# Sliding-window attention and a gated layer on one core: k's transposing DMA directly behind q's, and v spread earlier on GpSimd

## The chip, the cores and the metric

The kernel runs on one core of a Trainium2 chip. The metric is the device time of one execution in microseconds, the median of several runs. TensorE is written PE in the profile, VectorE DVE, ScalarE ACT, GpSimd POOL, and the queue from which SyncE issues DMAs SPq.

## The reference, cut to what matters

```python
# q, k, v: (8, 8, 576, 64) float32;  w_in: (512, 2048);  w_out: (2048, 512)
scores = q @ k.transpose(0, 1, 3, 2) / sqrt(64)
scores = where(0 <= row - column < 64, scores, -1e9)   # a causal window of 64
attn = exp(scores - max); attn = attn / (sum(attn) + 1e-9)
x = (attn @ v).transpose(0, 2, 1, 3).reshape(4608, 512)
h = x @ w_in
out = (h * cos(h)) @ w_out
```

There are eight batches of eight heads. Each row of 576 sees only itself and the 63 rows ahead of it, so attention is done in blocks of 64 rows (nine to a batch, numbered j = 0 to 8), each against 128 columns.

## The kernel before, in words

The second part, the layer, sets the shape. The 4608 rows of x are cut into nine row tiles of 512, numbered `mt`; each is one stage of the program. A stage has two halves. In the first, 16 column blocks `ff` of h are made by 64 matmuls (L359); ScalarE takes the sine of each (`sin`, L504) and VectorE multiplies it with h (`gT`, L507). In the second, 64 matmuls with w_out (L519) make the output (`out_ps`), which VectorE and ScalarE copy and SyncE stores.

Attention is threaded through these stages, one batch ahead. A planner holds a list of steps with due times: `at(time, function, ...)` enters one, and `pump(time)` emits all steps that are due, in order of time. A stage is T = 32 units of that time: the first 16 are one for each `ff`, the other 16 one for each four matmuls of the output. The due times decide only the order in which instructions stand in each engine's queue; on the chip every engine takes its queue in order, and semaphores hold an instruction until what it reads is there.

For batches b = 2 to 7 (t0 = 32(b - 1) is the start of the stage in which batch b's scores are made), the steps that matter here are these:

- `load_chunk` (L146): GpSimd issues the loads of q and of k, five chunks each, one stage ahead.
- `turn` (L213): SyncE issues a transposing DMA which turns the loaded rows of q or k (two of them: chunks 0 to 3, and chunk 4) into `qX` and `kX`, with the head dimension on the partitions.
- `spread_q` (L221): VectorE copies `qX` in four pieces into `qB`, a block layout with zeros between the two heads of a pair.
- `load_v` (L152): GpSimd issues five loads of v at the head of the stage.
- `spread_v` (L112, tile `v`): GpSimd makes, in two copies, the tiles of v that begin at odd multiples of 64.
- the scores of a group of 3 or 4 blocks (L263, tile `s_ps`) on TensorE, from about 14.6 units into the stage; then maximum on VectorE (L286), exponential on ScalarE (L297), reciprocal `rden` on VectorE (L304), the normalised weights `w` on GpSimd (L311), and a transposing DMA `wT` on SyncE (L323). There are 10 groups in a stage, 12 in the first.
- `values` (L338, tile `o_ps`) and `put_x` (tile `xT`) at the end of the stage: they use the weights of the blocks that belong to the next row tile, and the next stage's h matmuls wait for `xT`. One of the four `xT` copies is ScalarE's.
- `clear` (L367): in the stage of batch 2 alone, GpSimd sets `qB`'s second buffer to zero in four pieces.

In this kernel the turn of q for b > 2 stands at t0 - 5.8, near the end of the stage ahead; that of k stands at t0 + 0.2. For b = 2 they stand at 18.6 and 32.2. `spread_q` begins at t0 + 4.2 and `spread_v` at t0 + 24.2, among the `w` products.

Of the kernel before, what the change touches and what calls it, by code (L numbers as in the profile page):

```python
# [58 lines left out]
def kernel(  # L59
# [326 lines left out]
    def at(time, fn, *args):  # L386
        plan.append((time, len(plan), fn, args))
# [25 lines left out]
    for b in range(1, B):  # L413
        t0 = T * (b - 1)
        if b == 1:
            for p in range(PAIRS):
                for lag, fn in ((0, tr_q), (0.01, tr_k), (0.02, put_q), (0.03, put_k)):
                    at(7 + 1.8 * p + lag, fn, b, p)
        else:
            for i, name in enumerate(("q", "k")):  # L420
                for c in range(NC):
                    at(4 + 0.5 * (c + NC * i) if b == 2 else t0 - T + 4.9 + 0.9 * (c + NC * i), load_chunk, name, b, c)
                for c, (lo, hi) in enumerate(((0, 4), (4, 5))):
                    at((t0 + 0.2 if i else 18.6 if b == 2 else t0 - 5.8) + 0.1 * c, turn, name, b, lo, hi)
            for c, (lo, hi) in enumerate(((0, 4), (4, 5))):
                for h in range(2):
                    at(t0 + 4.2 + h + 2 * c, spread_q, b, h, lo, hi)
            for c in range(5):
                at(t0 + 0.4 + 0.9 * c, load_v, b, c)
            for half in range(2):  # L430
                at(t0 + 24.2 + 0.1 * half, spread_v, b, half)
    for half in range(2):
        at(17.5, spread_v, 1, half, "dma")
    for p in range(PAIRS):
# [32 lines left out]
    turn, turn_h = iter(range(100)), iter(range(100))  # L467
# [17 lines left out]
    for mt in range(n_mt):  # L485
# [23 lines left out]
        half = n_ff // 2 if mt == 0 else n_ff  # L509
# [49 lines left out]
```

## Time and profile before

| what | value |
|---|---|
| median of 3 runs | 349.0 us (347.15 to 350.04) |
| the profiled execution | 350.49 us, its span 348.7 us |
| mean granted TensorE clock | 0.961 of full speed |
| PE busy | 306.8 us, 88% of the span |
| ACT busy | 238.0 us, 68% |
| DVE busy | 225.2 us, 65% |
| POOL busy | 194.1 us, 56% |
| HBM read and written | 36.70 MB and 9.44 MB |

The span runs from the first to the last instruction of the profiled execution; 1.8 us of its time lie outside it. Busy time on an engine does not say that the engine is what everything waits for: the four engines are interlocked, and the stages have different limits. In rows of a timeline the bracket at the end gives the time for which the engine sat idle ahead of that row and what released it; "x4" says that several like instructions are merged in one row.

### The profile page before, as it was taken

To read this page: it belongs to the slowest core of one execution; us is meant where nothing else is said; L and a number is where in the kernel's file an instruction comes from. 1 tells how busy PE (TensorE), PEld (TensorE's weight loads), DVE (VectorE), ACT (ScalarE), POOL (GpSimd) and SP (SyncE) were. 2 spreads that over 40 slices of the span, in tenths; PEclk is the share of its full clock that TensorE was granted. 3 is DMA by queue.
4 is the path that set the end of the run, shared out by engine and by line. 5 is a ranking of instruction groups with operands and counts; after the bars stand their busy time and mean duration, and the time that the engine had idled before them with its cause. 6 is when DMAs were issued, how large, how long until landed. Compare 5 with 4: busy or idle time off the path is not lost.

```text
span 348.7 us, 7499 instructions
## 1 busy us (share of the span) xinstructions
PE 306.8 (88%) x2452; PEld 153.7 (44%) x2452; DVE 225.2 (65%) x850; ACT 238.0 (68%) x785; POOL 194.1 (56%) x215
## 2 busy tenths in 40 slices
PE   3989999899988599928998299956999999999996
PEld 2644554435543255404553155423554545454443
DVE  5876897698669275935769166772759867723821
ACT  4897799569967498735977279763987998513610
POOL 9993176896898079922898049950791292000000
PEclk9989999999999899987999799996999999999999
DMA  7999999999399945999399992999369535111002
GB/s 95 179 210 207 187 163 126 104 200 170 61 133 158 223 58 104 117 154 184 65 118 144 163 133 58 148 157 207 65 57 198 157 60 137 50 62 61 0 33 89
DMA packets 165960, 43.56 MB, mean 125 GB/s; under 512 B 155104, under 2 KB 161440, under 8 KB 165920
## 3 DMA queue, kind: packets, MB, share of 16 engines
q0 software_dynamic: 99632, 18.36, 70.6%
q1 hardware_dynamic: 66144, 24.52, 36.8%
q8 instruction: 19, 0.31, 0.4%
q14 instruction: 21, 0.17, 0.2%
q10 hardware_dynamic: 144, 0.20, 0.2%
HBM read 36.70 MB, written 9.44 MB: 132 GB/s over the span
## 4 chain that ended last, share of the span: by engine, by line
PE 46%; DMA 18%; POOL 15%; DVE 9%; issue 8%; ACT 3%; POOLq 0%; SPq 0%; DVEq 0%
PE out_ps L519 22%; PE h_ps L359 17%; DMA kX<-k 11%; POOL w L311 5%; DMA v<-in_v_dram 4%; POOL v L112 4%; DVE gT L507 2%; PE s_ps L263 2%; ACT e L297 2%; POOL v L152 2%; DVE s L286 1%; DMA k<-in_k_dram 1%; DMA wT<-w 1%; PE o_ps L338 1%; POOL q L146 1%
## 5 line engine op out<-in xcount | busy, mean ns | idle before, releaser
L519 PE MATMUL out_ps<-w_out,gT 128*128 128x512 bf16 x560 | 139.2, 392 | 0.0
L359 PE MATMUL h_ps<-xT,w_in 128*128 128x512 bf16 x576 | 129.2, 382 | 1.5 <-DVE xT L112 0.6
L297 ACT ACTIVATE e<-s,negm 128x128 f32<-128x128 f32 x256 | 98.8, 390 | 30.7 <-DVE negm L286 30.7
L311 POOL TENSOR_TENSOR w<-e,rden 128x512 bf16<-128x512 f32 (+1 forms) x75 | 70.4, 955 | 76.6 <-DVE rden L304 73.2
L507 DVE TENSOR_TENSOR gT<-h_ps,sin 128x512 bf16<-128x512 f32 x144 | 93.3, 690 | 26.6 <-ACT sin L504 26.2
L504 ACT ACTIVATE sin<-h_ps 128x512 f32<-128x512 f32 x144 | 83.1, 598 | 39.4 <-PE h_ps L359 36.9
L286 DVE CUSTOM_DVE_ANT_0 s<-s_ps,mask 128x128 f32<-128x128 f32 x256 | 59.1, 286 | 42.3 <-PE s_ps L263 40.5
L359 PEld LDWEIGHTS <-w_in 128*128 128x128 bf16 x576 | 55.8, 98 | 67.6 <-issue 3.5
L519 PEld LDWEIGHTS <-gT 128*128 128x128 bf16 x560 | 53.2, 101 | 53.5 <-issue 6.3
L297 ACT ACTIVATION_READ_ACCUMULATOR e<-s,negm 128x1 f32 x256 | 48.5, 189 | 0.0
L263 PE MATMUL s_ps<-kX,qB 128*128 128x128 bf16 x216 | 23.1, 228 | 27.6 <-DMA kX<-k 27.6
L263 PEld LDWEIGHTS <-qB 128*128 128x128 bf16 x216 | 17.7, 102 | 43.7 <-DMA kX<-k 29.5
L152 POOL DMA_DIRECT2D v<-in_v_dram x40 | 34.1, 871 | 3.5 <-DMA k<-in_k_dram 1.9
L146 POOL DMA_DIRECT2D q<-in_q_dram x30 | 27.9, 956 | 9.1 <-PE h_ps L359 4.6
L112 ACT COPY out_sb<-out_ps 128x512 f32<-128x512 f32 (+1 forms) x18 | 10.3, 571 | 28.4 <-PE out_ps L519 22.9
L112 DVE CAST xT<-o_ps 128x512 bf16<-128x512 f32 x27 | 17.6, 681 | 17.8 <-PE o_ps L338 17.8
L146 POOL DMA_DIRECT2D k<-in_k_dram x30 | 25.3, 860 | 5.6 <-DMA q<-in_q_dram 3.9
L112 POOL COPY v<-v 64x2048 bf16<-64x2048 bf16 (+1 forms) x13 | 22.3, 1717 | 0.4
L286 DVE DVE_READ_ACCUMULATOR2_ANT negm<- 128x1 f32 x256 | 21.3, 83 | 0.0
L304 DVE RECIPROCAL rden<-den 128x4 f32<-128x4 f32 (+1 forms) x80 | 13.8, 172 | 11.1 <-ACT e L297 10.4
L112 DVE COPY out_sb<-out_ps 128x512 f32<-128x512 f32 x18 | 12.4, 690 | 13.1 <-PE out_ps L519 13.0
L221 DVE COPY qB<-qX 64x2048 bf16<-64x2048 bf16 (+1 forms) x24 | 16.4, 685 | 0.4
(53 smaller groups left out, 168.0 us busy)
## 6 DMA issues: line engine op xcount, KB each, us to landing
out_dram<-out_sb SPq DMA_DIRECT2D x16, 512.0 KB, 7.3
v<-in_v_dram POOLq DMA_DIRECT2D x32, 128.0 KB, 5.9
q<-in_q_dram POOLq DMA_DIRECT2D x24, 128.0 KB, 8.0
k<-in_k_dram POOLq DMA_DIRECT2D x24, 128.0 KB, 11.0
w_out<-in_moe_w_out_dram POOLq DMA_DIRECT2D x2, 1024.0 KB, 17.0
w_in<-in_moe_w_in_dram POOLq DMA_DIRECT2D x2, 768.0 KB, 12.7
wT<-w SPq DMA_TRANSPOSE x66, 2.5
out_dram<-out_sb SPq DMA_DIRECT2D x3, 256.0 KB, 2.0
```

The source lines that it names most:

```text
L112: {"a": nc.scalar.copy, "p": nc.gpsimd.tensor_copy}.get(engine, nc.vector.tensor_copy)(out, in_)
L146: nc.gpsimd.dma_start(out=st[name, b][:n, c].rearrange("p (h d) -> p h d", h=H), in_=src.rearrange("h p d -> p h d"))
L152: nc.gpsimd.dma_start(out=vt.rearrange("p (h d) -> p h d", h=H), in_=v[b, :, c * 128:c * 128 + n, :].rearrange("h p d -> p h d"))
L221: nc.vector.tensor_copy(to.rearrange("d (m i) t -> d m i t", i=n), of[d, lo:hi, :, 0:64 * n].rearrange("d c a (i t) -> d (c a) i t", i=n))
L263: nc.tensor.matmul(out=s_ps[:, u].rearrange("p (a t) -> p a t", a=2), lhsT=q_block(b, p, j), rhs=k_blocks(b, p, j), start=True, stop=True, ...
L286: nc.vector.tensor_tensor_reduce(out=s[:, u], in0=s_ps[:, u], in1=mask[:, 2 - j % 2 if j else 0], scale=-scale if b else -1.0, scalar=BIG, ...
L297: nc.scalar.activation(e[:, u], s[:, u], AF.Exp, bias=negm[:, u:u + 1], scale=1.0 if n < n_first else -1.0, accum_out=den[:, u:u + 1])
L311: (nc.gpsimd if engine == "p" else nc.vector).tensor_tensor(out=w[:, 0:u], in0=e[:, 0:u], op=ALU.mult, in1=rden[:, 0:u].unsqueeze(2).to_br ...
L359: nc.tensor.matmul(out=st["h", ff], lhsT=w_in_sb[:, ks, ff * 128:ff * 128 + 128], rhs=st["xT", mt][:, ks], start=start, stop=stop)
L504: nc.scalar.activation(sin, h_ps, AF.Sin, bias=math.pi / 2.0)
L507: nc.vector.tensor_tensor(out=gt[:, e], in0=h_ps, in1=sin, op=ALU.mult)
L519: nc.tensor.matmul(out=o_ps[e], lhsT=gT[ff // 2][:, ff % 2, ms * 128:ms * 128 + 128], rhs=w_out_sb[:, ff], start=ff == 0, stop=ff == n_ff - 1)
```

## The change

The turn of k is entered 0.2 after that of q, where it stood 6 units (for b = 2, 13.6) after it; for b = 2 both now stand at t0 - 2. `spread_q` moves back by 4 units, and `spread_v` moves forward from 24.2 to 14.

```diff
                 for c, (lo, hi) in enumerate(((0, 4), (4, 5))):
-                    at((t0 + 0.2 if i else 18.6 if b == 2 else t0 - 5.8) + 0.1 * c, turn, name, b, lo, hi)
+                    at(t0 - (2 if b == 2 else 5.8) + 0.2 * i + 0.1 * c, turn, name, b, lo, hi)
             for c, (lo, hi) in enumerate(((0, 4), (4, 5))):
                 for h in range(2):
-                    at(t0 + 4.2 + h + 2 * c, spread_q, b, h, lo, hi)
+                    at(t0 + 8.2 + h + 2 * c, spread_q, b, h, lo, hi)
             for c in range(5):
                 at(t0 + 0.4 + 0.9 * c, load_v, b, c)
             for half in range(2):
-                at(t0 + 24.2 + 0.1 * half, spread_v, b, half)
+                at(t0 + 14 + 0.1 * half, spread_v, b, half)
```

The queues of PE and ACT keep their order. In each stage, SyncE's queue has the two turns of k ahead of three or four `wT` (for b = 2, one) that stood ahead of them (and, for b = 2, the turns of q behind five `wT` that stood behind them). VectorE has its four `qB` copies between products 10 and 13 of the stage where they stood between products 6 and 9. GpSimd has its two copies of v directly behind the loads, ahead of all ten `w`; they stood behind five or six of them.

## The prediction, as it was put on record before the changed kernel ran

> **What bounds the kernel now.** I read the page first, then the busy time of each engine by stage, then the timeline of PE, then those of the queues that feed it. The page:
>
> ```profile
> span 348.7 us, 7499 instructions
> PE 306.8 (88%) x2452; PEld 153.7 (44%) x2452; DVE 225.2 (65%) x850; ACT 238.0 (68%) x785; POOL 194.1 (56%) x215
> PEclk9989999999999899987999799996999999999999
> ```
>
> PE is the nearest to full, and it idles for 348.7 - 306.8 = 41.9 us. Cutting the span where the h matmuls of each stage begin shows where:
>
> ```profile
> core 0: us, PE busy (x) PEld busy (x) DVE busy (x) ACT busy (x) POOL busy (x), PEclk, DMA share, GB/s
> 65.08:98.32 33.24, 31.02 (x231) 15.34 (x226) 25.78 (x108) 27.64 (x95) 29.12 (x31) 1.00 1.25 136
> 98.32:136.06 37.74, 32.43 (x233) 16.03 (x229) 24.66 (x108) 26.63 (x94) 25.00 (x27) 0.95 1.24 137
> 136.06:176.65 40.59, 32.84 (x229) 16.13 (x229) 24.86 (x109) 27.73 (x95) 25.69 (x27) 0.92 1.33 127
> 176.65:217.57 40.92, 32.89 (x228) 16.13 (x228) 24.88 (x109) 27.72 (x95) 25.81 (x28) 0.92 1.40 128
> 217.57:257.78 40.21, 33.62 (x228) 16.40 (x228) 24.71 (x109) 27.84 (x95) 25.77 (x28) 0.92 1.20 130
> 257.78:288.73 30.95, 30.93 (x228) 15.62 (x228) 24.32 (x109) 26.93 (x95) 16.56 (x18) 1.00 0.91 131
> ```
>
> These are the stages mt = 1 to 6, with batch 2 to 7 in them. All hold the same PE work, yet mt = 6 takes 30.95 us with PE never idle and mt = 2 to 5 take 38 to 41 at a lower clock. Stage 6 differs in having no loads of q and k (POOL 16.56 against about 25.7). The first score matmuls of the stages mt = 2 to 6 in PE's timeline:
>
> ```profile
> 117.58 0.50 PE L263 MATMUL s_ps<-kX,qB 128*128 128x128 bf16 x3 [5.28 <-DMA kX<-k]
> 157.80 0.61 PE L263 MATMUL s_ps<-kX,qB 128*128 128x128 bf16 x4 [7.72 <-DMA kX<-k]
> 198.69 0.60 PE L263 MATMUL s_ps<-kX,qB 128*128 128x128 bf16 x4 [8.01 <-DMA kX<-k]
> 238.17 0.61 PE L263 MATMUL s_ps<-kX,qB 128*128 128x128 bf16 x4 [6.57 <-DMA kX<-k]
> 271.59 0.39 PE L263 MATMUL s_ps<-kX,qB 128*128 128x128 bf16 x4
> ```
>
> Four waits, 27.6 us, all for the turned k. PE reaches the scores 13.8 us into the stage (271.59 - 257.78) and finds no `kX`. Each wait costs more than its length, as the five microseconds behind one show in the granted clock (0.65):
>
> ```profile
> 157.80:162.80 5.00, 5.00 (x25) 2.48 (x26) 1.86 (x17) 2.18 (x11) 0.00 (x0) 0.65 1.58 269
> ```
>
> Why `kX` is late stands in SyncE's queue and in GpSimd's (the rows are of stage mt = 3, from 136.06 on). The last three rows are of the DMA view: the median time from issue to landing of the two turns of k in mt = 3, then mt = 1, then mt = 6:
>
> ```profile
> 135.75 3.56 SPq L213 DMA_TRANSPOSE qX<-q  x2
> 139.42 4.05 SPq L323 DMA_TRANSPOSE wT<-w  x3
> 143.65 9.04 SPq L213 DMA_TRANSPOSE kX<-k  x2
> ...
> 137.15 4.26 POOL L152 DMA_DIRECT2D v<-in_v_dram  x5
> 153.46 0.69 POOL L146 DMA_DIRECT2D k<-in_k_dram  x1 [1.81 <-DMA q<-in_q_dram]
> ...
> kX<-k SPq DMA_TRANSPOSE x2, 10.6
> kX<-k SPq DMA_TRANSPOSE x2, 7.3
> kX<-k SPq DMA_TRANSPOSE x2, 3.5
> ```
>
> k's turn is issued 7.6 us into the stage, behind three `wT`, amid the 15 loads that GpSimd issues from 137.15 to 154.15. Its first part takes from 143.65 until PE starts at 157.80. Without loads of q and k beside it (mt = 6) the turn lands in 3.5 us. In mt = 1 it is issued here:
>
> ```profile
> 67.06 4.10 SPq L213 DMA_TRANSPOSE kX<-k  x1
> ```
>
> That is 2.0 us into its stage, beside the same number of loads; it lands in 7.3, and PE does not wait.
>
> **The change, part by part.** *k's turn.* The work is the same (two DMAs a stage); the place moves. Past three `wT` it gains the 4.2 us from 139.42 to 143.65. The second gain comes by way of GpSimd (mt = 4):
>
> ```profile
> 169.93 3.41 POOL L112 COPY v<-v 64x1536 bf16<-64x1536 bf16 x2
> 173.42 4.39 POOL L311 TENSOR_TENSOR w<-e,rden 128x384 bf16<-128x384 f32 x5
> ```
>
> q's turn stands behind the sixth `wT`, which needs the `w` at 173.42, held by the two copies of v ahead of it. With these gone that `w` follows its `rden`, up to 3.4 us earlier, and both turns move up with it. In a stage of 31 us I place k's turn by the rows of mt = 6, where the sixth `rden` (the second of three blocks) is done at
>
> ```profile
> 282.95 0.18 DVE L304 RECIPROCAL rden<-den 128x3 f32<-128x3 f32 x1 [0.77 <-ACT e L297]
> ```
>
> 25.3 into the stage. Add 0.8 for the `w`, 1.3 for the `wT`, 3.6 for q's turn and, in three stages, another `wT`: k's turn goes out at 31.0 to 32.3, that is 0 to 1.5 us into the next stage. The nearest landing is mt = 1's, 7.3 us; with that it lands at 7 to 9, with the worst (14.1) at 14 to 16, against a need at 13.8. I take the first: no wait. What this returns is the stage's excess over 30.95: 6.79 + 9.64 + 9.97 + 9.26 = 35.7 us for mt = 2 to 5. The `wT` that now stand behind k's turn are groups 7 to 10, whose blocks are used a whole stage later: nothing.
>
> *q's turn for batch 2* held five `wT` (SyncE's queue first, then PE):
>
> ```profile
> 51.03 7.17 SPq L213 DMA_TRANSPOSE qX<-q  x2
> 58.25 8.59 SPq L323 DMA_TRANSPOSE wT<-w  x6
> ...
> 62.14 0.32 PE L338 MATMUL o_ps<-wT,v 128*64 128x64 bf16 x8 [0.88 <-DMA wT<-w]
> 97.88 0.51 PE L338 MATMUL o_ps<-wT,v 128*64 128x64 bf16 x20 [1.57 <-DMA wT<-w]
> ```
>
> Now they go first, and the 0.88 goes. The price: q's turn lands inside stage 1, and the spread behind it must not stall VectorE. Its place moves from about 6 to 10 us into the stage; issued at about 63.4, the turn lands by 71 if it takes the 7.3 of k's. Nothing.
>
> *`spread_v`* no longer delays the sixth `w` of mt = 1, whose `wT` the row at 97.88 waits for: 1.57 less. Its new place is ahead of the first `w`, which in the stages mt = 2 to 6 is ready some 18 us in, while the loads end at 14 to 18 (153.46 + 0.69 is 18.1 in the worst of them). The 3.41 us lie in idle time, or at the worst end at 21.5; the ten `w` then run back to back at 0.95 and the sixth is ready at 27.2, 1 us behind its row of mt = 6. If that cover goes, the values of mt = 2 and 3 (which need six groups; later ones four) wait for it. The DMA view gives the landing of two `wT` beside the loads (137 to 141 us), and of the ten of mt = 5:
>
> ```profile
> wT<-w SPq DMA_TRANSPOSE x2, 7.7
> wT<-w SPq DMA_TRANSPOSE x10, 2.5
> ```
>
> I put 0.5 on each of the two boundaries, as by then the loads are mostly through; the bounds are 0 and 7.7 - 2.5 = 5 each.
>
> *`spread_q`* is 1.8 us of VectorE in four copies, four products later. It has fewer products left in which to catch up: a product takes 0.69, PE gives one each 0.87. Stretched copies are the risk:
>
> ```profile
> 72.82 1.48 DVE L221 COPY qB<-qX 64x2048 bf16<-64x2048 bf16 x1
> 264.39 0.68 DVE L221 COPY qB<-qX 64x2048 bf16<-64x2048 bf16 x1
> 272.42 0.69 DVE L507 TENSOR_TENSOR gT<-h_ps,sin 128x512 bf16<-128x512 f32 x1 [0.17 <-ACT sin L504]
> 288.60 0.58 ACT L112 CAST xT<-o_ps 128x512 bf16<-128x512 f32 x1
> ```
>
> The first ran beside a memset on GpSimd (mt = 1), the second with GpSimd idle. In mt = 6 the last product (272.42) had caught up. With the spreads at 10 to 14 us it ends 0.2 to 0.8 later, and the maxima and exponentials behind it start up to 0.6 later. ScalarE is full from there to its `xT` copy, which ends at 289.18, while PE wants it after three matmuls of 0.22 behind 288.73, at 289.38: 0.2 of slack. I charge 0.3 a stage, six times: 1.8. Bounds: 0, and 1.5 a stage (9 in all) if every copy stretches as at 72.82.
>
> The Trainium skill ("SBUF — State Buffer", Who interferes with whom) says that VectorE in its two-port mode and GpSimd exclude each other for a whole instruction, whichever starts first. The pair 1.48 against 0.68 agrees. By that rule a v copy that starts ahead of a `qB` copy would hold it for its whole length; it speaks against bringing the two together. By the rule, with a collision in every stage, the sum would be that of rival B below; by the rows, which place the two some microseconds apart, the one that follows.
>
> *The sum*, on the profiled execution: 350.49 - 35.7 - 0.9 - 1.6 + 1.0 + 1.8 = 315.1. The median of the runs lies 1.5 under that execution: 313.7, said as 314.
>
> **The rivals.**
>
> (A) *k's turn is still late.* What the queue alone gives is 4.2 us; the loads begin at 1.1 us into the stage (137.15) either way. DMA is busy for most of a stage:
>
> ```profile
> DMA  9095999999999999999999999900606325330013
> ```
>
> This is mt = 5 in 40 slices of 1.005 us; about 28 us of work, which must fit in 31. If the turn keeps its 14 us, the waits become 0, 3.5, 3.8 and 2.4, and by proportion (9.64 lost for 7.72 waited) about 12 us return: 314 + 12 = 326. Against it: the landing in mt = 1. The Trainium skill ("DMA: Bandwidth & Descriptors", Queues, rings and completion order) has each DMA engine alternate between its queues packet by packet; by that the turn beside loads should take about twice its 3.5, 7 us, and A would be unlikely. The 7.3 agrees, the 10.6 and 14.1 do not.
>
> (B) *GpSimd or its port becomes the bound.* The copies of v meet the spreads of q, or push the `w` back: 1.5 us in six stages, 9, so 323. For it: the stretched copy; against it: the loads end behind 14 us, when the spreads are nearly over.
>
> (C) *Slower.* The longest landing of a load of k:
>
> ```profile
> DMA to landing us min/median/max: 2.3/9.6/17.7
> ```
>
> SyncE now meets k's turn early and must wait at the head of its queue for the loads of k, which in a shorter stage land later. It decides from the point where `kX` lands more than 21.7 us into the stage (157.80 - 136.06). Loads issued until 18.1 with 17.7 end at 35.8, 4.9 into the next; with 14.1 for the turn that is 19. Three more in each of four stages are needed; at 25 us the loss is 3.3 a stage with its slow clock on top, some 16: 365. A long stage also gives the loads time again.
>
> **How the numbers follow.** Forecast 0.64 (309 to 320); A 0.18; B 0.12; C 0.04; 0.02 for anything else. Without any cost the lowest run gives 347.15 - 38.2 = 309, so the low end is 308; A and B both reach to 326. One per cent, 3.5 us, is about what a measurement of this kernel tells from no change; the forecast, A and B all lie beyond it: faster 0.94, same 0.02, slower 0.04.
>
> **What would show it.** Right: no row of PE that waits for `kX`; the stages mt = 1 to 5 at 31 to 32 us with clock 1.00; k's turn issued within 2 us of the stage's start; GpSimd's copies of v ahead of the first `w`. A shows as waits of 2 to 4 us for `kX`, with landings over 10; B as `qB` copies over 1 us or `o_ps` waiting for `wT`; C as SyncE waiting for loads of k ahead of L213. Wrong outright: stages as short as 31 us in which another wait of several microseconds appears, which would mean that the work hidden behind the waits for `kX` was itself near the limit.

## The result, and the profile after

The changed kernel takes 321.24 us in the median of four runs (319.62 to 326.39), the kernel before 349.52 beside it (347.15 to 351.41): a ratio of 0.918, with a 95% interval of 0.910 to 0.926. Two later series gave 320.23 and 320.16, a ratio of 0.913 both times (0.907 to 0.919 and 0.908 to 0.919). The first profiled execution was the longest of its four; the rows below are from a second one, of 318.38 us, which stands 2 to 3 us below the medians. The page of the changed kernel:

```profile
span 316.6 us, 7499 instructions
PE 298.3 (94%) x2452; PEld 150.6 (48%) x2452; DVE 223.8 (71%) x850; ACT 236.8 (75%) x785; POOL 193.9 (61%) x215
PEclk9979999999999999999999999999999999999999
```

PE idles for 18.3 us where it idled for 41.9, the slices with a clock below 9 in the middle of the span are gone, and PE's own busy time is 8.5 us less for the same matmuls. The same six stages, mt = 1 to 6, in the view of busy time by stretch (columns as in the prediction):

```profile
63.17:96.28 33.11, 30.62 (x230) 15.26 (x226) 25.38 (x108) 27.05 (x94) 29.12 (x31) 1.00 1.48 159
96.28:127.23 30.95, 30.93 (x228) 15.62 (x228) 23.82 (x109) 26.92 (x95) 25.91 (x27) 1.00 1.55 162
127.23:159.47 32.24, 31.10 (x228) 15.53 (x229) 24.05 (x107) 26.77 (x93) 25.44 (x27) 1.00 1.65 163
159.47:191.81 32.34, 31.27 (x229) 15.54 (x229) 24.31 (x107) 27.49 (x95) 25.41 (x27) 1.00 1.52 165
191.81:223.76 31.95, 31.26 (x228) 15.52 (x228) 24.44 (x107) 27.50 (x95) 25.41 (x27) 1.00 1.56 164
223.76:256.57 32.81, 31.41 (x229) 15.59 (x229) 26.01 (x109) 27.89 (x97) 17.59 (x17) 1.00 0.90 121
```

Stages mt = 2 to 5 lost 32.0 us together (159.46 before, 127.48 now). Stage 1 is as long as it was (33.11 against 33.24), and stage 6, the undisturbed one before, is 1.86 longer. With the 1.9 us by which stage 1 begins earlier (63.17 against 65.08) that makes, to 0.1, the 32.1 us between the two profiled executions. The reason is in SyncE's queue (timeline of the changed kernel):

```profile
68.52 5.67 SPq L213 DMA_TRANSPOSE kX<-k  x2
...
116.23 9.47 SPq L323 DMA_TRANSPOSE wT<-w  x7
126.30 3.48 SPq L213 DMA_TRANSPOSE qX<-q  x2
130.01 5.54 SPq L213 DMA_TRANSPOSE kX<-k  x2
...
140.82 1.28 SPq L382 DMA_DIRECT2D out_dram<-out_sb  x2
```

In mt = 3 k's turn is issued 2.8 us into the stage, where it was 7.6; in mt = 2, 4 and 5 it is 1.2, 3.5 and 4.2 (97.51, 162.93 and 196.03), where it was 7.8, 8.2 and 8.8. In all four it now goes out ahead of the loads of q and k that GpSimd issues in the stage. What is left over 30.95 a stage has names too, in PE's timeline:

```profile
79.12 0.40 PE L263 MATMUL s_ps<-kX,qB 128*128 128x128 bf16 x4 [2.00 <-DMA kX<-k]
...
150.45 0.40 PE L263 MATMUL s_ps<-kX,qB 128*128 128x128 bf16 x4 [1.11 <-DVE negm L286]
160.68 4.69 PE L359 MATMUL h_ps<-xT,w_in 128*128 128x512 bf16 x21 [0.40 <-ACT xT L112]
239.42 0.38 PE L263 MATMUL s_ps<-kX,qB 128*128 128x128 bf16 x4 [0.68 <-DVE gT L507]
```

One wait for `kX` is left, in mt = 1. In mt = 3 PE now waits for a maximum (`negm`) of VectorE (0.64 and 0.26 us in the next two stages), at the head of mt = 4 for ScalarE's `xT`, in mt = 6 for a product. Why VectorE is late (timelines of VectorE and GpSimd):

```profile
148.80 0.69 DVE L112 COPY out_sb<-out_ps 128x512 f32<-128x512 f32 x1 [2.73 <-DMA out_dram<-out_sb]
...
234.77 3.93 POOL L112 COPY v<-v 64x1536 bf16<-64x1536 bf16 x2 [5.19 <-DMA v<-in_v_dram]
237.58 1.19 DVE L221 COPY qB<-qX 64x256 bf16<-64x256 bf16 x1
239.40 0.22 DVE L221 COPY qB<-qX 64x256 bf16<-64x256 bf16 x1
```

The first row is a wait that the profile before does not have: the copy of an output tile needs a buffer whose store has not landed. The other rows are of mt = 6: a small `qB` copy takes 1.19 us beside GpSimd's copy of v and 0.22 alone. The view of DMA for mt = 3 (the first row is the busy share of the 16 DMA engines in 40 slices, the others end with the median us from issue to landing; the last row is the first of the turn's two DMAs alone, the one for which the scores wait):

```profile
DMA  7996999999999999999999999999999999994935
out_dram<-out_sb SPq DMA_DIRECT2D x2, 512.0 KB, 8.4
kX<-k SPq DMA_TRANSPOSE x2, 9.4
kX<-k SPq DMA_TRANSPOSE x1, 10.8
```

The stores issued at 140.82 take 8.4, so they land at about 149, when the copy at 148.80 starts; the maxima behind it are late, and PE waits at 150.45. In a stage of 32 us the DMA engines are busy for 90% or more of the time in 35 of 40 slices. And the waits of the changed kernel as a whole (us in total, times, longest):

```profile
DVE out_sb L112 <- DMA out_dram<-out_sb: 7.6, 4, 2.7
PE s_ps L263 <- DMA kX<-k: 2.0, 1, 2.0
```

### The profile page after: what moved, and what is told of

Its sections match the earlier page's. It is cut to its first block, busy times and chain, and to the rows that moved or that the text cites. A ratio compares the mean times of both kernels' runs of the same rounds, so it can differ in the third digit from the quotient of the medians.

```text
span 324.6 us, 7460 instructions
## 1 busy us (share of the span) xinstructions
PE 298.6 (92%) x2413; PEld 151.7 (47%) x2452; DVE 224.9 (69%) x850; ACT 237.2 (73%) x785; POOL 192.8 (59%) x215
## 4 chain that ended last, share of the span: by engine, by line
PE 58%; ACT 13%; DMA 13%; DVE 9%; issue 4%; POOL 1%; DVEq 0%; POOLq 0%; ACTq 0%
PE h_ps L359 33%; PE out_ps L519 18%; ACT e L297 10%; DMA out_dram<-out_sb 8%; DMA kX<-k 3%; DVE s L286 3%; DMA k<-in_k_dram 2%; PE o_ps L338 1%; PE s_ps L263 1%; DVE gT L507 1%; ACT out_sb L112 1%; DVE w L311 1%; PE out_ps L374 1%; DVE qB L221 1%; PE s_ps L272 1%
## 5 line engine op out<-in xcount | busy, mean ns | idle before, releaser
L519 PE MATMUL out_ps<-w_out,gT 128*128 128x512 bf16 x543 | 132.6, 384 | 1.4 <-issue 0.7
L359 PE MATMUL h_ps<-xT,w_in 128*128 128x512 bf16 x557 | 127.9, 381 | 4.5 <-ACT xT L112 2.0
L507 DVE TENSOR_TENSOR gT<-h_ps,sin 128x512 bf16<-128x512 f32 x144 | 94.5, 688 | 30.4 <-ACT sin L504 30.0
L519 PEld LDWEIGHTS <-gT 128*128 128x128 bf16 x560 | 52.2, 99 | 51.2 <-issue 2.2
L286 DVE CUSTOM_DVE_ANT_0 s<-s_ps,mask 128x128 f32<-128x128 f32 x256 | 58.4, 285 | 9.2 <-PE s_ps L263 7.5
L146 POOL DMA_DIRECT2D k<-in_k_dram x30 | 26.2, 888 | 8.9 <-DMA v<-in_v_dram 6.7
L146 POOL DMA_DIRECT2D q<-in_q_dram x30 | 25.5, 897 | 9.3 <-DMA w_out<-in_moe_w_out_dram 9.3
L263 PE MATMUL s_ps<-kX,qB 128*128 128x128 bf16 x216 | 22.3, 222 | 7.7 <-DMA kX<-k 3.8
L304 DVE RECIPROCAL rden<-den 128x4 f32<-128x4 f32 (+1 forms) x80 | 13.8, 173 | 16.7 <-ACT e L297 15.7
L221 DVE COPY qB<-qX 64x2048 bf16<-64x2048 bf16 (+1 forms) x24 | 14.5, 606 | 0.4
```

The source lines that it names most:

```text
L146: nc.gpsimd.dma_start(out=st[name, b][:n, c].rearrange("p (h d) -> p h d", h=H), in_=src.rearrange("h p d -> p h d"))
L221: nc.vector.tensor_copy(to.rearrange("d (m i) t -> d m i t", i=n), of[d, lo:hi, :, 0:64 * n].rearrange("d c a (i t) -> d (c a) i t", i=n))
L263: nc.tensor.matmul(out=s_ps[:, u].rearrange("p (a t) -> p a t", a=2), lhsT=q_block(b, p, j), rhs=k_blocks(b, p, j), start=True, stop=True, ...
L286: nc.vector.tensor_tensor_reduce(out=s[:, u], in0=s_ps[:, u], in1=mask[:, 2 - j % 2 if j else 0], scale=-scale if b else -1.0, scalar=BIG, ...
L359: nc.tensor.matmul(out=st["h", ff], lhsT=w_in_sb[:, ks, ff * 128:ff * 128 + 128], rhs=st["xT", mt][:, ks], start=start, stop=stop)
L507: nc.vector.tensor_tensor(out=gt[:, e], in0=h_ps, in1=sin, op=ALU.mult)
```

## The experiments

The theory under test had two parts. First, `kX` was late because its turn ran beside the loads of q and k on full DMA engines, and the change takes it ahead of them. Second, the time by which the forecast was missed lies in the DMA engines too, as these now have 31 us for a stage's work. The rivals were that the position in SyncE's queue alone decides, that the late stores by themselves cost the rest, and that engines (VectorE and GpSimd) do.

**The changed kernel as it is**, for a second profile and as the measure for the others of its series.

> The changed kernel once more, for its profile beside the other runs of this call. Theory (DMA): the time not won, some 7 us of the forecast 314, sits in three places of the first profile: stage mt = 1 at 36.7 us (kX waited for, 2.88, because both turns of batch 2 now run among the loads), mt = 4 and 5 at 34.4 and 33.6 (VectorE's out_sb copy waits 3.9 and about 3.4 for the last stage's store to land), mt = 6 at 32.6 (qB copies beside GpSimd's v copies). Expected 319 to 322 with the same three places. Rival (disturbed run): the first profile, at 326.4, was taken of an odd execution, and a profile near 320 shows stages mt = 4 and 5 near 32 with no wait for a store.

320.23 us (318.38 to 322.41), ratio 0.913 (0.907 to 0.919); its rows stand above. The three places are there again, smaller: stage 1 takes 33.1 us, stages 4 and 5 take 32.3 and 32.0 with store waits of 2.2 and 1.7, and stage 6 takes 32.8.

**The turn of k alone.**

```diff
 (kernel before)
-at((t0 + 0.2 if i else 18.6 if b == 2 else t0 - 5.8) + 0.1 * c, turn, name, b, lo, hi)
+at(t0 - (2 if b == 2 else 5.8) + 0.2 * i + 0.1 * c, turn, name, b, lo, hi)
```

> Only the turns move; the spreads of q and of v stay where they were. Theory (the turn is what counts): the waits for kX in mt = 2 to 5 go and most of the gain is here: 322 to 328, a few us above the changed kernel since the two copies of v still hold back the sixth w and with it q's and k's turn by up to 3.4 us. Rival (the two moves need each other): the turn stays stuck behind the sixth wT, kX lands after 14 us into the stage, and less than half of the 28 us is won: above 335.

328.88 us (327.63 to 330.21), ratio 0.938 (0.932 to 0.944): most of the gain, 0.9 above the range of the theory. Timelines of GpSimd, SyncE and PE around stage 4 (which begins at 165.64), then its waits:

```profile
158.92 3.41 POOL L112 COPY v<-v 64x1536 bf16<-64x1536 bf16 x2
162.41 4.39 POOL L311 TENSOR_TENSOR w<-e,rden 128x384 bf16<-128x384 f32 x5
169.80 6.86 SPq L213 DMA_TRANSPOSE kX<-k  x2
181.58 0.40 PE L263 MATMUL s_ps<-kX,qB 128*128 128x128 bf16 x4 [1.91 <-DMA kX<-k]
...
PE s_ps L263 <- DMA kX<-k: 7.9, 4, 3.1
```

The wait for `kX` falls from 27.6 us to 7.9. The copies of v still hold back the `w` on which q's turn waits, and k's turn goes out 4.2 us into this stage and 6.9 into the next, where the wait is the longest.

**The copies of v alone.**

```diff
 (kernel before)
-at(t0 + 24.2 + 0.1 * half, spread_v, b, half)
+at(t0 + 14 + 0.1 * half, spread_v, b, half)
```

> Only GpSimd's copies of v move. Theory (the turn is what counts): SyncE reaches q's and k's turns up to 3.4 us earlier, but k's still stands behind three or four wT and among the loads; PE's waits for kX shrink by 1 to 3 us each: 338 to 347. Rival (v alone does most): 330 or less. Second rival (hidden anyway): 348 to 351.

339.86 us (339.39 to 343.57), ratio 0.971 (0.964 to 0.979). Timelines of SyncE and PE (the stage's h matmuls begin at 175.00), then the waits:

```profile
175.00 14.02 PE L359 MATMUL h_ps<-xT,w_in 128*128 128x512 bf16 x64
181.36 6.27 SPq L213 DMA_TRANSPOSE kX<-k  x2
192.58 0.61 PE L263 MATMUL s_ps<-kX,qB 128*128 128x128 bf16 x4 [3.56 <-DMA kX<-k]
...
PE s_ps L263 <- DMA kX<-k: 17.6, 4, 5.8
```

k's turn still goes out 6.4 us into the stage. The two edits are worth 21.5 and 10.5 us by themselves and 30.1 together (350.35 - 320.23, with `spread_q` moved as well): they nearly add up, as the prediction had it, which let both shift one and the same issue.

**A third output buffer.** This takes away what makes VectorE wait for the store.

```diff
 (changed kernel)
-o_sb = moe.tile([128, 2, d_model], F32, tag="out", name="out_sb", bufs=2)
+o_sb = moe.tile([128, 2, d_model], F32, tag="out", name="out_sb", bufs=3)
```

> The changed kernel with three buffers for out_sb in place of two, the order of all queues unchanged: VectorE's first out copy of a stage need not wait for the store of the stage ahead. Theory (DMA, stores): the waits of 3.9 and 3.4 us in mt = 4 and 5 go, these stages fall to about 31.7 from 34.4 and 33.6, and the time to about 316. Rival (ScalarE is the limit): the exponentials fill ScalarE to the end of the stage, what VectorE waited was slack, and the time stays within 1 us of the changed kernel's.

321.93 us (318.63 to 325.06), ratio 0.915 (0.907 to 0.923): no gain. The waits of the profiled execution (325.06 us), then GpSimd's and SyncE's rows behind the longer one:

```profile
PE s_ps L263 <- DMA kX<-k: 9.4, 2, 6.5
...
145.97 0.69 POOL L146 DMA_DIRECT2D k<-in_k_dram  x1 [2.58 <-DMA q<-in_q_dram]
150.16 6.60 POOL L311 TENSOR_TENSOR w<-e,rden 128x512 bf16<-128x512 f32 x7
166.04 7.78 SPq L213 DMA_TRANSPOSE kX<-k  x2
```

No wait of VectorE for a store is left, and the stages mt = 3 and 5 take 31.2 and 31.3 us (32.2 and 32.0 in the changed kernel). But mt = 4 takes 39.8: PE waits there 6.5 us for `kX` (the other 2.9 are in mt = 1). The rows show the path. In mt = 3, which begins at 128.26, GpSimd issues the last load of k 17.7 us into the stage, behind a wait for a load of q. The copies of v stand behind it until 150.08, seven `w` follow back to back, the `wT` follow these, and k's turn goes out 6.6 us into mt = 4 (159.41). So the copies of v, which the change put behind the loads, hand a late load on to the turns of the next stage. That removing the store wait lowers the time does not hold. That the stage is short of DMA time, and that whichever transfer is last in it shows the wait, fits this run; whether its other executions have such a stage is not shown.

**The kernel before without the loads of q and k** of batches 3 to 7, which reuse those of batch 2.

```diff
 (kernel before, load_chunk)
+if b > 2:
+    st[name, b] = st[name, 2]
+    return
```

> The kernel before, without the loads of q and k for batches 3 to 7 (the turns read batch 2's rows again; everything else, the place of the turns too, as before). Theory (DMA: k's turn is late because it shares the DMA engines with those loads, its place in SyncE's queue costs little): kX lands in 3 to 5 us, PE does not wait for it, the stages mt = 2 to 5 fall from 38 to 41 to about 31, and the time to 312 to 318, as low as the changed kernel or lower. Rival (queue: the turn is late since it stands behind three wT and the copies of v hold those back): it still goes out 7 us into the stage, with q's turn late as well, and waits of several us for kX remain: 330 or more.

317.03 us (316.57 to 320.82), ratio 0.904 (0.898 to 0.911). Timelines of SyncE and PE in one stage, its landing in the view of DMA, and the waits (line numbers are 3 higher here):

```profile
128.94 13.97 PE L362 MATMUL h_ps<-xT,w_in 128*128 128x512 bf16 x62
137.27 6.27 SPq L216 DMA_TRANSPOSE kX<-k  x2
...
kX<-k SPq DMA_TRANSPOSE x2, 4.8
...
PE s_ps L266 <- DMA kX<-k: 1.7, 2, 1.6
```

k's turn is still issued 8.3 us into the stage, behind the `wT`, yet it lands in 4.8 us instead of 10.6, and 1.7 us of waiting are left of 27.6. In mt = 2, 4 and 5 the same median is 3.6, 3.9 and 3.8, where it was 9.1, 11.1 and 9.3. So its place in the queue was costly only because of the loads that run beside it from there; and as the changed kernel shows, an earlier place beside the same loads ends nearly all of the waiting too.

**The changed kernel without these loads.**

```diff
 (changed kernel, load_chunk)
+if b > 2:
+    st[name, b] = st[name, 2]
+    return
```

> The changed kernel, without the loads of q and k for batches 3 to 7 (the turns read batch 2's rows again). Theory (DMA is what fills the changed kernel's stages): the waits for kX in mt = 1 and those of out_sb for the stores go, the stages mt = 1 to 5 take 31.0 to 31.4, and the time is 311 to 314, some 8 us under the changed kernel; against the kernel before without these loads the change is worth 3 us or less. Rival (engines: what is left is VectorE's, ScalarE's and GpSimd's own work): 317 or more.

320.25 us (320.08 to 321.27), ratio 0.912 (0.908 to 0.915): as long as with the loads, and longer than the kernel before without them. Timelines of GpSimd and VectorE, and the waits:

```profile
140.66 3.41 POOL L112 COPY v<-v 64x1536 bf16<-64x1536 bf16 x2 [6.94 <-DMA v<-in_v_dram]
142.83 1.32 DVE L224 COPY qB<-qX 64x256 bf16<-64x256 bf16 x1
...
PE s_ps L266 <- DVE gT L510: 3.9, 6, 0.7
```

With nothing of q and k to issue, GpSimd comes to its copies of v as soon as v has landed, and there they meet the `qB` copies in every stage, as in mt = 6 of the changed kernel. The theory's 311 to 314 is missed. That the meeting pays for the DMA work taken away is tested further down, where the spreads are moved as well.

**The turns of batch 2 apart**, q's back to where it was and k's late in the stage ahead.

```diff
 (changed kernel)
-at(t0 - (2 if b == 2 else 5.8) + 0.2 * i + 0.1 * c, turn, name, b, lo, hi)
+at((18.6 + 11.6 * i if b == 2 else t0 - 5.8 + 0.2 * i) + 0.1 * c, turn, name, b, lo, hi)
```

> The changed kernel with the turn of q for batch 2 at 18.6 again, ahead of the five wT of its stage; k's turn of batch 2 stays at 30.2 and all else as changed. Theory (stage 1 lost its time because two turns in place of one now run beside its loads): k's turn goes out some 3 to 4 us earlier, the wait of 2.0 to 2.9 us for kX in mt = 1 goes, but the wait for a wT at the end of stage 0 (0.88 in the kernel before) comes back: 1 to 2 us faster than the changed kernel. Rival (the loads alone set when kX lands): the wait for kX stays, and with the wait for wT the kernel is 1 us slower than the changed one.

321.47 us (318.85 to 326.77), ratio 0.912 (0.905 to 0.919). In the profiled execution (326.77 us) the wait for `kX` in mt = 1 is gone, but PE waits for `wT` three times, 3.6 us in all; the longest is in its timeline at the end of stage 0:

```profile
65.90 0.41 PE L338 MATMUL o_ps<-wT,v 128*64 128x64 bf16 x14 [2.16 <-DMA wT<-w]
```

The `wT` for the values stand behind the turn again. The expected gain of 1 to 2 us is not there. Stages 0 and 1 take 75.3 us together in this profile, and 70.3 to 73.9 in three of the changed kernel; the intervals of the whole time overlap.

**`spread_q` where it was.**

```diff
 (changed kernel)
-at(t0 + 8.2 + h + 2 * c, spread_q, b, h, lo, hi)
+at(t0 + 4.2 + h + 2 * c, spread_q, b, h, lo, hi)
```

> The changed kernel with the four copies of q's spread at t0 + 4.2 again. Theory (late spreads cost what the prediction charged): ScalarE's xT copy is in time again, four waits of 0.4 us go, the qB copies of mt = 6 no longer run beside GpSimd's copies of v and that stage falls from 32.7 to about 31; but the qX of batch 2, turned inside stage 1, lands after the spreads' place there, so VectorE waits in mt = 1: together within 2 us of the changed kernel. Rival (the spreads were moved for nothing): 3 us or more faster. Second rival (needed everywhere): qX is late in each stage and the kernel is slower by 5 us or more.

319.68 us (315.32 to 321.02), ratio 0.911 (0.906 to 0.916). The waits:

```profile
DVE out_sb L112 <- DMA out_dram<-out_sb: 5.0, 3, 3.3
PE h_ps L359 <- ACT xT L112: 0.6, 2, 0.4
```

At the heads of mt = 4 to 6 the changed kernel has three waits for `xT` of 0.4 us; here one is left. Stage 6 falls to 31.06 us; the wait for the store stays. The interval overlaps that of the changed kernel, so a gain is not shown. It is not excluded either: two of the four runs, 315.32 and 318.38, are no longer than the shortest of the changed kernel (318.38).

**Without the loads, and `spread_q` where it was.** Both suspected costs, DMA work and the meeting of copies, are taken away together.

```diff
 (changed kernel without the loads of q and k)
-at(t0 + 8.2 + h + 2 * c, spread_q, b, h, lo, hi)
+at(t0 + 4.2 + h + 2 * c, spread_q, b, h, lo, hi)
```

> The changed kernel without the loads of q and k for batches 3 to 7 (the turns read batch 2's rows again) and with q's spreads at t0 + 4.2. Theory (without the loads GpSimd reaches its copies of v 10 us into the stage and they meet VectorE's qB copies; that meeting made after_no_loads slow, at 320.3): the qB copies fall from up to 1.3 us to 0.7 and 0.2, PE no longer waits for gT, the stages mt = 2 to 6 take 30.9 to 31.1, and the time is 311 to 314. Rival (the changed place of the turns or of v costs something else): it stays at 317 or more.

313.30 us (311.01 to 314.73), ratio 0.891 (0.886 to 0.897). One stage of it (columns as above), and VectorE's and GpSimd's timelines in it:

```profile
125.25:156.22 30.97, 30.72 (x225) 15.63 (x230) 24.33 (x109) 27.30 (x95) 17.06 (x17) 1.00 0.86 129
...
134.51 0.21 DVE L224 COPY qB<-qX 64x256 bf16<-64x256 bf16 x1
135.99 3.41 POOL L112 COPY v<-v 64x1536 bf16<-64x1536 bf16 x2 [5.38 <-DMA v<-in_v_dram]
```

This stage is at the 30.95 on which the forecast was built (the one behind it at 30.95 too), the `qB` copy is at 0.21, and the whole time is the forecast's. The 6.9 us to the changed kernel (320.16 in this series) go only when both are taken away: leaving out the loads alone gives 320.25, the spreads alone 319.68. That fits two limits of nearly the same height. That the loads' part is their DMA work is argued: leaving them out also frees GpSimd's queue earlier.

**Stores issued earlier**, ahead of the work that fills the DMA engines.

```diff
 (changed kernel)
-at(t0 + 8.2 + h + 2 * c, spread_q, b, h, lo, hi)
+at(t0 + (8.2 if b == 2 else 4.2) + h + 2 * c, spread_q, b, h, lo, hi)
...
-at(base + T + (0.5 if mt else 7) + ms0 / 2, store, o_sb, mt, ms0, 0, 2)
+at(base + (T - 7 + ms0 * 3.6 if mt else T + 7 + ms0 / 2), store, o_sb, mt, ms0, 0, 2)
```

> The changed kernel with the first store of each stage mt = 1 to 7 issued 25 units into its own stage, ahead of the turns, in place of 32.5, and with q's spreads at t0 + 4.2 except for batch 2. Theory (stores land too late for the next stage's first out copy): VectorE's waits for a store, 5 to 8 us in all, go, the meeting with the copies of v in mt = 6 goes, and the time falls 3 to 6 us under the changed kernel, to 314 to 317. Rival (DMA is full: what one transfer wins another loses): the wait for kX comes back in mt = 3 to 5, or wT is waited for, and the time stays within 2 us of the changed kernel.

321.04 us (316.59 to 322.84), ratio 0.910 (0.902 to 0.918). The waits of the profiled execution (322.84 us):

```profile
PE s_ps L263 <- DMA kX<-k: 7.1, 3, 3.5
```

The store wait is gone and waits for `kX` stand in its place, 3.5 us in mt = 3 and 1.0 in mt = 4 (the third is that of mt = 1, 2.6): much as with the third buffer, brought about in another way. This other order of the same transfers did not help.

**The changed kernel once more**, beside these two.

> The changed kernel as it is, for comparison on this chip: 319 to 322, with VectorE's waits for a store and the 2 us for kX in mt = 1 as in its other profiles.

320.16 us (318.69 to 322.40), ratio 0.913 (0.908 to 0.919).

**Without the stores of row tiles 1 to 6**, `spread_q` where it was: less DMA work of another kind.

```diff
 (changed kernel with spread_q at t0 + 4.2)
-if mt < n_mt - 1:
+if mt < 1 or mt == n_mt - 2:
     at(base + T + (0.5 if mt else 7) + ms0 / 2, store, o_sb, mt, ms0, 0, 2)
```

> spread_q_back without the stores of row tiles 1 to 6 (1 MB a stage; these rows of the output are not written), the loads of q and k kept. Theory (the sum of DMA work is what fills a stage of 31 us, whichever transfer carries it): with 3 of some 29 us of DMA work gone, the waits for a store and, from mt = 2 on, for kX go, the stages mt = 2 to 6 take 31.0 and the time is 313 to 316, about that of no_loads_q_back (313.3). Rival (it is the many small packets of the loads that matter, and a store has few): waits for kX of 1 to 4 us stay in one or two stages, and the time stays at 317 or more.

316.70 us (314.37 to 322.04), ratio 0.902 (0.894 to 0.910). The waits:

```profile
PE s_ps L263 <- DMA kX<-k: 2.4, 3, 1.0
```

The time goes the way the theory says, by 3.0 us against the 319.68 with the stores, but it ends between the two expectations, and the intervals (0.894 to 0.910, 0.906 to 0.916) overlap: inconclusive by itself.

No kernel that computes the whole is measurably faster than the changed one; `spread_q` where it was comes nearest.

## Why the prediction was right, and where its terms were off

*What bounds the kernel.* Right. The four waits for `kX` and the clock behind them were the time: stages 2 to 5 gave back 32.0 of the 35.7 us of that term.

*k's turn.* Right in effect, but both numbers behind it were too small. It was to go out 0 to 1.5 us into the stage and to land at 7 to 9; it goes out at 1.2, 2.8, 3.5 and 4.2 in mt = 2 to 5. And the 7.3 us to its landing were the median of the turn's two DMAs, while the scores wait for the first: that one took 8.2 in mt = 1 of the kernel before, and the 10.6 and 14.1 that the prediction sets side by side are the median and the first DMA of one and the same turn. In the changed kernel the first takes 8.3, 10.8, 9.8 and 9.7. So in mt = 3 it lands 13.6 us into the stage (130.01 + 10.8 - 127.23) against a need at 13.8, and in mt = 5 at 13.9 against 14.4: 0.2 and 0.5 us are to spare where the prediction's numbers left nearly 5. That PE does not wait there is close to luck. In the first execution it does, in mt = 4, by 0.94 us.

The q turn of mt = 3 goes out 0.9 us ahead of the stage, not the 2 to 3.5 of the prediction's sum: SyncE issues seven `wT` back to back until then (9.47 us from 116.23, 1.35 each), and the prediction costed only the last one or two. The turns of mt = 4 and 5 go out later still: in mt = 3 the sixth `w` is done 28.3 us into the stage (155.48), where the prediction's sum has 26.1, and VectorE's wait of 2.73 us for a store stands ahead of it. Both edits move that one issue, as the two runs with one edit each show: 4.2 and 6.4 us into mt = 4.

*Why 7.3 and not 14 us of landing.* The prediction chose the landing of mt = 1, as the nearest row, and could not say why the turn took longer elsewhere. The kernel before without the loads shows it: at nearly the same place in the queue the median is 3.6 to 4.8 in mt = 2 to 5 without the loads of q and k, and 9.1 to 11.1 beside them, 2.2 to 2.8 times as long. In the three profiles of the changed kernel it is 6.6 to 9.4 in mt = 1 to 5. The rule of the Trainium skill that was weighed there ("DMA: Bandwidth & Descriptors", Queues, rings and completion order) gave about 7, twice the 3.5. The measurement decides: 1.9 to 2.7 times the 3.5, so twice is the low end.

*"q's turn for batch 2 ... Nothing."* This step failed. The turn was followed to VectorE's spread, but not to what stands behind it in SyncE's queue, k's turn: that went from 67.06, 2.0 us into stage 1, to 68.52, 5.4 us into it, and lands behind the start of the scores. The gain of 1.6 at the end of stage 1 is real (the waits have no row of values for `wT`), but the wait of 2.00 for `kX` takes it back: 33.11 where the terms add up to 31.9. The run with the turns of batch 2 apart shows that the other order has its own price.

*`spread_v`.* The ten `w` behind the copies kept up in this execution; the charge of 1.0 for the values of mt = 2 and 3 was not needed, as no such wait is in the trace. The prediction let a late `w` cost the values alone, though; the run with the third buffer shows it reach k's turn. In mt = 6 the step failed. Its cover, the loads of q and k in GpSimd's queue, is not there in that stage, the copies run 11 us in, and the `qB` copies are stretched beside them: rival B, in one stage of six, which is 1.9 us longer (0.4 of it the wait for `xT`) where B was priced at 1.5. The changed kernel without the loads extends the same to every stage. The exclusion that the Trainium skill states ("SBUF — State Buffer", Who interferes with whom) agrees: 1.32 us beside GpSimd's copy, 0.21 alone, and the longer one ends at 144.15, when GpSimd's pair is through (144.07).

*`spread_q`.* The charge of 0.3 a stage through ScalarE's `xT` was met in kind: PE waits 0.4 at the heads of mt = 4, 5 and 6 (160.68 is the first), 1.2 us where 1.8 was charged. With `spread_q` where it was, one of the three is left, so most of it hangs on this move.

*The term that was missing.* "Wrong outright" was to be stages near 31 us in which another wait of several microseconds appears. A small form of it is there: the output copy waits for the store in mt = 2 to 5, 7.6 us on VectorE, of which PE sees 1.11, 0.64 and 0.26 in the last three (which are 0.5 to 1.1 a stage beyond the terms). The prediction counted 28 us of DMA work against a stage of 31 for rival A alone and took it as fitting. It fits, but not each transfer in time: in the profiles with a third buffer and with earlier stores the wait moves to `kX`, and with the loads out and the copies apart the stages are at 30.95. That the DMA engines are the shared limit fits all these; which transfer slows which was not measured by itself, and the run without stores leaves the size of their part open.

*The sum.* Against its terms, the part ahead of stage 1 is 1.0 us better and stage 2 0.8, stage 1 is 1.2 worse, stages 3 to 5 together 2.3 and stage 6 1.6: 3.3 us in all, 318.38 for the profiled execution against 315.1. The rest, up to 320 to 321, lies between executions. The first one (326.39 us) shows where: 36.77 us in stage 1 (64.63 to 101.40) and 34.41 in stage 4, with these rows of PE and VectorE:

```profile
81.44 0.61 PE L263 MATMUL s_ps<-kX,qB 128*128 128x128 bf16 x4 [2.88 <-DMA kX<-k]
178.96 0.40 PE L263 MATMUL s_ps<-kX,qB 128*128 128x128 bf16 x4 [0.94 <-DMA kX<-k]
187.23 0.69 DVE L112 COPY out_sb<-out_ps 128x512 f32<-128x512 f32 x1 [3.87 <-DMA out_dram<-out_sb]
```

They are the waits for `kX` in mt = 1 and for the store, longer, and one more for `kX`, in mt = 4. The median was taken 1.5 below the profiled execution, as before; here it is 2 to 3 above the second one. So the 321.24 stands 7 us above the 314, and above the 309 to 320 of the forecast itself; it lies within the whole range because that reached up to the rivals' 326. The gain was forecast at 35 us and is 28.3: the mechanism was right, and the landing, the turn for batch 2 and DMA time were taken too lightly.

*The rivals and the signs.* A stayed out of mt = 2 to 5 in the second execution, narrowly, and shows in mt = 1 and in mt = 4 of the first; B came in one stage; C did not: no wait of SyncE for a load of k appears. Of the signs, the clock of 1.00 and the copies of v ahead of the first `w` are there; k's turn within 2 us of the stage's start is there in mt = 2 alone, and stages of 31 to 32 us in mt = 2 and 5, with mt = 3 and 4 at 32.2 and 32.3.

## What to carry to other kernels

When a wait of several microseconds in each stage is to go, work out every shared resource for the stage that will remain, the DMA engines too, and ask of each transfer how far its landing is from its first use; the one with the least slack is the next wait. Where a step moves in a queue, follow what now stands behind it as far as what moved, and look at each stage in which the cover is different (here the first and the last). Take the landing of the transfer that the engine waits for, not the median over several. A transfer's place in the queue and the traffic beside it are two causes: leaving out the traffic tells them apart in one run.

## What was not expected of the hardware

The turn of k takes 3.5 us from issue to landing in stage 6 of the kernel before, 3.6 to 4.8 in stages 2 to 5 without the loads of q and k, and 6.6 to 11.6 in the stages 1 to 5 of all profiles with them (medians of its two DMAs): traffic on another queue makes it two to three times as long. And a `qB` copy of 64x256 goes from 0.21 to 1.32 us beside a copy on GpSimd, six times as long. GpSimd's pair beside it took the 3.41 that it takes alone in that stage, and up to 4.20 in the others of that run.
